# Weight sums in eight wide GpSimd operations a pair instead of twelve narrow ones, four exponential buffers, and scores issued two steps ahead of outputs

## The chip, the cores and the metric

The kernel runs on one core of a Trainium2 chip. The metric is the device time in microseconds (us) of one execution; for before it is the median of three runs, 595.99 us (595.43 to 596.42).

## The reference

Windowed attention with memory keys, followed by a two-layer feed-forward network, all in 32-bit floats:

```python
batch, n_heads, seq, head_dim = (4, 8, 768, 64)      # n_mem = 8
chunk, left_ctx, right_ctx = (32, 16, 8)
for c in range(seq // chunk):                        # 32 queries see 56 keys and 8 memory keys
    scores = scale * q_c @ k_full^T
    scores = scores - max(scores)
    a = exp(scores); a = a / (sum(a) + 1e-9)
    out[c] = a @ v_full
x = out.transpose(0, 2, 1, 3).reshape(3072, 512)
h = x @ w_in                                         # w_in 512 x 2048
g = max(h, 0) + alpha * min(h, 0)
return g @ w_out                                     # w_out 2048 x 512
```

## The kernel before, in words

**Blocks and units.** The 3072 tokens are eight blocks of 384. A block has four pairs of heads, and a (block, pair) is a *unit*; there are 32. A unit goes through: *scores* (TensorE, tile `s_ps`, L346), the row maximum (VectorE, `mx`, L369 and L372), six exponentials (ScalarE, `e`, L380), the denominator (VectorE, `den`, L395 and L398), a multiplication by its inverse (GpSimd, `e<-e,den`, L401), a ScalarE copy (`e2`, L405), fourteen 32-row transposes (VectorE, `pt`, L422), and *outputs* (TensorE, `a_ps`, L445), whose result becomes rows of x. Units 0 to 7 (blocks 0 and 1) go through a denser form of this at the start. The 24 others go two at a time, through the function `attend`.

**Full precision.** Every 32-bit factor of the feed-forward part is split into a rounded part ("high", a ScalarE copy) and the rest ("low", a subtraction), and a product is three TensorE products. So every hidden slice needs a `high` and a `low` before TensorE can use it.

**Places.** Blocks 0 and 1 are computed plainly. There are 32 *places*: one of the two blocks and one of the 16 slices f of the hidden width. A place has an `up` (12 products into `h_ps`, L760; two such buffers, so the `up` of place p needs place p-2 to have been read), a bend (ScalarE L769, then VectorE `g<-g,rise,h_ps`, L772), the split of the hidden slice (ScalarE `xh<-g` L778 and the subtraction `xl<-g,xh` or `gl<-g,gh`, L782), and a `down` (9 products into `o_ps`, L790). TensorE runs the `down` of a place after the `up` of the second place behind it. Places 0 to 17 alternate between the blocks, slices 0 to 8; place 18 is slice 9 of block 0, place 23 slice 14, place 24 slice 15; places 25 to 31 are slices 9 to 15 of block 1. Each slice's weights are first decoded, on ScalarE and VectorE: `w_t<-w_t` copies (L677) and shifts (L681), `a<-a,w_t` (L685), and the low part `w<-a,w` (L698), all 1024 elements a partition.

**Blocks 2 to 7** go in three big stages of two blocks. A 2x2 product is done with seven sub-products (L1139) of sums of blocks of x (`xf`; L931, L935, L949) and sums of blocks of w_in. The latter are made once, early, by `put_far`, on GpSimd, for each of the eight pairs of slices, and stored in device memory as `far_a` and `far_b`, with copies of the weights themselves; `load` brings them back for each stage. In `put_far` L870 adds high and low parts, L873 adds and subtracts quarters, ScalarE rounds (L877), L880 forms the low part, and SyncE stores.

**What sets the order.** Nothing is scheduled on the chip: each engine runs its own queue in order and waits on semaphores. The queues are written by a planner (`Plan`) when the program is built: each step is given an engine, a cost and a due time (`rest`), and the planner lists the steps by them. Costs and due times thus move instructions without changing what they do. `BEGIN` gives the places at which `attend` is called for units 8 and up, `AT_PAIR` and `AT_REST` the points in the big stages; `FIRST_SLOW` is the first place whose low part is made on GpSimd instead of VectorE.

Of the kernel before, what the change touches and what calls it, by code (L numbers as in the profile page):

```python
# [100 lines left out]
FIRST_SUM, SUM_EVERY = 9, 3  # L101
FIRST_SLOW = 20
# [8 lines left out]
DUE_WEIGHTS = 4  # L111
# [77 lines left out]
def body(ctx: ExitStack, tc: tile.TileContext, qvw, kw, whole, heads, w_in, w_out, alpha, out):  # L189
# [73 lines left out]

    def due(u, later=0):

        return rest(begins(u) + later + (5.5 if u >= FIRST_FRONT else 0))
# [4 lines left out]

    def e_keys(u):
        return [("e", u % 2, n) for n in range(NJ * 2)]

    def den_keys(u):
        return [("den", u % 3, n) for n in range(NJ * 2)]
# [83 lines left out]
    def scores(us):  # L360
# [57 lines left out]
    def turn(u):  # L418
# [125 lines left out]
    def windows(u):  # L544
# [20 lines left out]
        def total():  # L565
            st["den"] = sm.tile([P, NJ * 2, 1], F32, name="den", tag=f"den{u % 3}")
# [93 lines left out]
    def decode_part(k, parts):  # L660
# [52 lines left out]
        step(POOL if late else DVE, 1.3 if late else 0.15 + 0.53 * n, low, reads=[a] + [("w", i, f, 0) for i in parts],  # L713
# [16 lines left out]
    def hidden(blk, f, first_f, last_f):  # L730
# [72 lines left out]
        def add_bend():  # L803
# [3 lines left out]
            step(*((POOL, 1.05) if slow else (DVE, 0.56)), low, reads=[sd, gh], writes=[gl] + new)  # L807
# [21 lines left out]
    MORE = PLACES + [(sums, f"s{i}", [("f", i, 0), ("f", i, 1)]) for i in range(4)]  # L829
# [31 lines left out]
    def put_far(i, place):  # L861
        f0, f1 = 2 * i, 2 * i + 1
        t = {}

        def w(f, hl, k2):
            return ws[f, 0][:, hl, k2 * HALF:(k2 + 1) * HALF]

        def full(n, f, k2):
            t[n] = sums.tile([P, HALF], F32, name="sum", tag=f"t{n}")
            nc.gpsimd.tensor_tensor(out=t[n], in0=w(f, 0, k2).bitcast(F32), in1=w(f, 1, k2).bitcast(F32), op=ALU.add)  # L870

        def merge(n, a, b, op):
            nc.gpsimd.tensor_tensor(out=t[n], in0=t[a], in1=t[b], op=op)  # L873

        def high(n, x):
            t["s", x] = sums.tile([P, 2, HALF], F32R, name="form", tag=f"s{x}")
            nc.scalar.copy(out=t["s", x][:, 0], in_=t[n])  # L877

        def low(n, x):
            nc.gpsimd.tensor_tensor(out=t["s", x][:, 1], in0=t[n], in1=t["s", x][:, 0].bitcast(F32), op=ALU.subtract)  # L880

        def put(x, to):
            nc.sync.dma_start(out=to.rearrange("p (l m) -> p l m", l=2), in_=t["s", x].bitcast(F32))

        def raw_sum(n, f, k2):
            step(POOL, 0.7, partial(full, n, f, k2), reads=[("gate", place - 1), ("w", 0, f, 0), ("w", 0, f, 1)], writes=[("t", n)])

        def add(n, a, b, op):
            step(POOL, 0.7, partial(merge, n, a, b, op), reads=[("t", a), ("t", b)], writes=[("t", n)])

        def form(n, x, to, key):
            step(ACT, 0.4, partial(high, n, x), reads=[("t", n)], writes=[("f", x, 0), ("f", x, 1)])
            step(POOL, 0.7, partial(low, n, x), reads=[("t", n), ("f", x, 0)], writes=[("f", x, 1)])
            step(SP, 0.7, partial(put, x, to), reads=[("f", x, 0), ("f", x, 1)], writes=[key])
# [115 lines left out]
    def big(s):  # L1010
# [228 lines left out]
        def meet(u, banks):  # L1239
# [206 lines left out]
```

## Time and profile before

| what | value |
| --- | --- |
| median of three runs | 595.99 us |
| the profiled execution, its own time | 596.48 us |
| its span, first to last instruction | 594.7 us |
| TensorE busy | 575.0 us (97%) |
| VectorE busy | 456.5 us (77%) |
| ScalarE busy | 302.2 us (51%) |
| GpSimd busy | 201.7 us (34%) |
| mean granted TensorE clock | 0.991 |

In the profile PE is TensorE, PEld its weight loads, DVE VectorE, ACT ScalarE, POOL GpSimd, SP SyncE. A row of the timeline gives start, duration, engine, line, operation, tiles, shape and count, and in brackets the idle time before it with what ended it. The profiled execution lies 0.5 us above the median of the runs; 1.8 us of its time lie outside the span.

### The profile page before, as it was taken

The page shows a single profiled execution, that of the slowest core. Times are in us where ns is not written, and L with a number is a line of the kernel's source. Part 1 is how long each engine was busy: PE and PEld are TensorE (multiplying, and loading weights), DVE is VectorE, ACT ScalarE, POOL GpSimd, SP SyncE. Part 2 cuts the span into 40 slices and gives each one's busy share as a digit, 9 for nine tenths or more (in the row PEclk, how much of TensorE's full clock was granted, in tenths as well). Part 3 has the DMA queues.
Part 4 walks back from the last instruction along what each step waited for, and adds up shares of the span by engine and source line. Part 5 has one row for each costly group of instructions (what it writes and reads, how often), then busy time and mean ns, then how long its engine had stood idle before and what let it go on. Part 6 is the DMA issues. An engine that isn't in the chain of part 4 may idle for free.

```text
span 594.7 us, 12044 instructions
## 1 busy us (share of the span) xinstructions
PE 575.0 (97%) x4467; PEld 508.3 (85%) x4467; DVE 456.5 (77%) x987; ACT 302.2 (51%) x796; POOL 201.7 (34%) x230
## 2 busy tenths in 40 slices
PE   7999999769999999999999999999999999999997
PEld 4888987658988889999888998999888999999886
DVE  7989999878687978798879688897959466566420
ACT  3887878553765553534654633536464433323421
POOL 5663395997699460001123500101212500000000
PEclk9999999897999999999999999999999999999999
DMA  8999746384698577677898886778797776776821
GB/s 317 398 418 416 304 178 244 110 311 181 210 372 346 170 266 262 245 293 265 329 354 285 285 309 230 252 252 311 288 301 272 224 272 209 259 280 243 316 92 53
DMA packets 44395, 159.41 MB, mean 268 GB/s; under 512 B 5040, under 2 KB 10416, under 8 KB 35632
## 3 DMA queue, kind: packets, MB, share of 16 engines
q1 hardware_dynamic: 44192, 158.51, 73.0%
q8 instruction: 35, 0.57, 0.4%
q14 instruction: 24, 0.20, 0.1%
q10 hardware_dynamic: 144, 0.13, 0.1%
HBM read 129.26 MB, written 29.36 MB: 267 GB/s over the span
## 4 chain that ended last, share of the span: by engine, by line
PE 75%; POOL 5%; DVE 4%; issue 1%; ACT 1%; POOLq 0%; ACTq 0%
PE b_ps L1071 33%; PE b_ps L1139 27%; PE o_ps L790 4%; PE h_ps L760 4%; PE a_ps L445 3%; PE b_ps L1107 2%; PE s_ps L346 2%; POOL form L880 2%; POOL sum L870 2%; POOL sum L873 1%; DVE xf L935 1%; DVE w L698 1%; DVE w_t L677 0%; DVE a L685 0%; DVE pt L422 0%
## 5 line engine op out<-in xcount | busy, mean ns | idle before, releaser
L1139 PE MATMUL b_ps<-xf,wa 128*128 128x384 f32 x924 | 172.7, 336 | 0.1
L1139 PEld LDWEIGHTS b_ps<-xf,wa 128*128 128x128 f32 x924 | 161.9, 188 | 7.0 <-ACT plain L519 0.7
L1159 DVE TENSOR_TENSOR u<-b_ps,u 128x384 f32<-128x384 f32 x154 | 82.7, 554 | 37.5 <-PE b_ps L1139 33.6
L422 DVE STREAM_TRANSPOSE pt<-e 32x64 f32<-32x64 f32 (+1 forms) x336 | 99.5, 301 | 14.8 <-POOL e L401 9.1
L1032 ACT ACTIVATE g<-u 128x384 f32<-128x384 f32 x88 | 45.8, 525 | 102.5 <-DVE u L1159 98.6
L1071 PE MATMUL b_ps<-wo,xh 128*128 128x512 f32 x276 | 86.0, 393 | 0.0
L1071 PE MATMUL b_ps<-wo,gh 128*128 128x512 f32 x276 | 85.6, 392 | 0.0
L401 POOL TENSOR_TENSOR e<-e,den 128x384 f32<-128x384 f32 x24 | 20.4, 850 | 141.3 <-DVE den L398 137.1
L760 PE MATMUL h_ps<-xh,w 128*128 128x384 f32 x256 | 66.9, 343 | 0.0
L1071 PEld LDWEIGHTS b_ps<-wo,gh 128*128 128x128 f32 x276 | 51.8, 188 | 9.9
L1071 PEld LDWEIGHTS b_ps<-wo,xh 128*128 128x128 f32 x276 | 51.8, 188 | 9.7
L790 PE MATMUL o_ps<-w,xh 128*128 128x512 f32 x168 | 53.9, 403 | 0.0
L1071 PE MATMUL b_ps<-wo,gl 128*128 128x512 f32 x138 | 53.9, 390 | 0.0
L1071 PE MATMUL b_ps<-wo,xl 128*128 128x512 f32 x138 | 53.9, 390 | 0.0
L760 PE MATMUL h_ps<-xl,w 128*128 128x384 f32 x128 | 45.1, 352 | 5.6 <-DVE g L772 5.6
L380 ACT ACTIVATE e<-s_ps,mx 128x64 f32<-128x64 f32 x144 | 43.2, 319 | 10.9 <-DVE mx L372 10.9
L760 PEld LDWEIGHTS h_ps<-xh,w 128*128 128x128 f32 x256 | 47.4, 192 | 1.3 <-DVE w L698 0.6
L949 POOL TENSOR_TENSOR plain<-plain 128x384 f32<-128x384 f32 x24 | 26.7, 1137 | 46.0 <-ACT plain L519 45.4
L880 POOL TENSOR_TENSOR form<-sum,form 128x256 fp32r<-128x256 f32 x32 | 32.1, 1026 | 29.0 <-ACT form L877 29.0
L790 PE MATMUL o_ps<-w,xl 128*128 128x512 f32 x84 | 34.3, 408 | 5.1 <-DVE xl L782 5.1
L790 PEld LDWEIGHTS o_ps<-w,xh 128*128 128x128 f32 x168 | 32.8, 195 | 6.5
L1035 DVE SCALAR_TENSOR_TENSOR g<-g,rise,u 128x384 f32<-128x384 f32 x44 | 28.2, 641 | 10.8 <-ACT g L1032 10.3
(112 smaller groups left out, 928.4 us busy)
## 6 DMA issues: line engine op xcount, KB each, us to landing
wo<-far_o SPq DMA_DIRECT2D x46, 1024.0 KB, 4.8
wa<-far_a SPq DMA_DIRECT2D x22, 1024.0 KB, 4.8
wa<-far_b SPq DMA_DIRECT2D x22, 768.0 KB, 5.8
w_t<-w_in SPq DMA_DIRECT2D x16, 512.0 KB, 9.7
w_t<-w_out SPq DMA_DIRECT2D x16, 512.0 KB, 9.3
far_o<-w SPq DMA_DIRECT2D x16, 512.0 KB, 4.8
qk<-kw SPq DMA_DIRECT2D x24, 272.0 KB, 6.4
v_t<-qvw SPq DMA_DIRECT2D x24, 256.0 KB, 6.2
```

The source lines that it names most:

```text
L380: nc.scalar.activation(out=st["e"][:, i], in_=st["s"][h2][:, n], func=AF.Exp, scale=SCALE, bias=d["mx"][:, u - us[0], n, h2:h2 + 1], accum ...
L401: nc.gpsimd.tensor_tensor(out=st["e"], in0=st["e"], in1=st["den"].broadcast_to([P, NJ * 2, KW]), op=ALU.mult)
L422: nc.vector.transpose(out=pts[u % NPT][quad * CH:(quad + 1) * CH, j, t0:t0 + n1 - n0].rearrange("p t h q -> p (t h) q"), in_=(st["e"], zer ...
L760: nc.tensor.matmul(out=h["ps"][:, :BT], lhsT=ws[f, 0][:, wk, k * P:(k + 1) * P], rhs=parts(blk, k)[1](xk), start=(k == 0 and n == 0), stop ...
L790: nc.tensor.matmul(out=o_ps[tt], lhsT=h[gk][:, tt * P:(tt + 1) * P], rhs=ws[f, 1][:, wk], start=(f == first_f and i == 0), stop=(f == last ...
L880: nc.gpsimd.tensor_tensor(out=t["s", x][:, 1], in0=t[n], in1=t["s", x][:, 0].bitcast(F32), op=ALU.subtract)
L949: step(POOL, 0.95, lambda: nc.gpsimd.tensor_tensor(out=plain_at(to[0]), in0=plain_at(a[0]), in1=plain_at(b[0]), op=ALU.subtract), reads=[a ...
L1032: nc.scalar.activation(out=h[name], in_=src(), func=AF.Relu, scale=-1.0)
L1035: nc.vector.scalar_tensor_tensor(out=to() if to else h[name], in0=h[name], scalar=rise[:, f:f + 1], in1=src(), op0=ALU.mult, op1=ALU.add)
L1071: nc.tensor.matmul(out=o[which][tt], lhsT=h[gk][:, tt * P:(tt + 1) * P], rhs=w[:, wk].bitcast(F32R), start=(f == turns[which][0] and i == ...
L1139: nc.tensor.matmul(out=h[bank[1]][:, :BT], lhsT=weight(wk, p).bitcast(F32R), rhs=xf[xi][:, xk, p], start=p == 0 and k == 0, stop=p == 1 an ...
L1159: nc.vector.tensor_tensor(out=h[t], in0=h[bank[1]][:, :BT], in1=h[t if of is None else of], op=ALU.add)
```

## The change

**Weight sums.** For one pair of slices, GpSimd did twelve operations of 256 elements a partition: four sums of high and low parts, four sums of quarters, four low parts. Now the sums of high and low parts and the low parts are taken over both halves at once: two of 512, four of 256, two of 512. ScalarE rounds twice 512 instead of four times 256, and SyncE stores two forms instead of four. The forms lie elsewhere in `far_a` and `far_b`, so one sub-product (T1) takes its weights from the second load and another (B22) from the first.

**Places.** The sums of the eight pairs began at places 9, 12, 15, ... 30; now they begin at 9, 11, 13, 18, 22, 26, 29 and 30. `FIRST_SLOW` goes from 20 to 14, so the low parts of places 14 to 19 move from VectorE to GpSimd. Some of the planner's costs are larger than they were.

**Attention.** The exponentials of units 8 and up get four buffers instead of two (denominators four instead of three). Scores of two units are issued two steps ahead of the outputs (news are units v+4 and v+5 where the outputs are of v and v+1), not one. A new table `END` gives the places of the outputs; the weights and transposes are due with it. In the first big stage one of the four slices ahead of the second `attend` is taken before it, not two.

```diff
-BEGIN = (20, 24, 28, 32, 36, 40.3, 48.2, 55.8, 59.8, 69.4, 77.3, 85)
-AT_PAIR = ({2: 18, 5: 20}, {3: 26, 6: 28}, {})
-AT_REST = ({2: 22, 11: 24}, {2: 30, 11: 32}, {})
+BEGIN = (20, 22, 25.5, 28.5, 32, 36.0, 44, 49.5, 55.8, 58.8, 66.4, 75.3)
+END = (25, 28.5, 32.5, 38.5, 46.5, 49.5, 54.8, 58.5, 65.4, 75.3, 81.5, 92.5)
+AT_PAIR = ({2: 16, 5: 18}, {1: 24, 3: 26}, {})
+AT_REST = ({3: 20, 8: 22}, {4: 28, 12: 30}, {})
...
-FIRST_SUM, SUM_EVERY = 9, 3
-FIRST_SLOW = 20
+SUM_AT = (9, 11, 13, 18, 22, 26, 29, 30)
+SPLIT = 1
+FIRST_SLOW = 14
...
+    def e_place(u):
+        return u % 2 if u < NWIN else u % 4
...
-        step(DVE, 0.14 + 0.28 * n, ends, writes=r)
-        step(DVE, 0.15 + 0.54 * n, join, reads=r, writes=[a])
+        step(DVE, 0.14 + (0.28 if f < 6 else 0.35) * n, ends, writes=r)
+        step(DVE, 0.15 + (0.54 if f < 6 else 0.6) * n, join, reads=r, writes=[a])
...
-        raw_sum(0, f0, 0)
-        raw_sum(1, f1, 0)
-        step(POOL, 0.7, lambda: ... merge(2, 0, 1, ALU.subtract), ...)
-        form(2, 0, b[:, :2 * HALF], ("db", i, 1))
-        raw_sum(3, f1, 1)
-        add(1, 1, 3, ALU.add)
-        form(1, 1, a[:, 6 * HALF:], ("da", i, 1))
-        add(0, 1, 0, ALU.subtract)
-        form(0, 2, a[:, 4 * HALF:6 * HALF], ("da", i, 2))
-        raw_sum(3, f0, 1)
-        add(3, 3, 0, ALU.subtract)
-        form(3, 3, b[:, 4 * HALF:], ("db", i, 2))
+        raw_sum(0)
+        raw_sum(1)
+        add((1, 1), (1, 0), (1, 1), ALU.add)
+        add((1, 0), (0, 0), (1, 0), ALU.subtract)
+        form(1, b[:, :4 * HALF], ("db", i, 1))
+        add((0, 0), (1, 1), (0, 0), ALU.subtract)
+        add((0, 1), (0, 1), (0, 0), ALU.subtract)
+        form(0, a[:, 4 * HALF:], ("da", i, 1))
...
-        def meet(u, banks):
-            olds, news = [u - 2, u - 1], [u, u + 1] if u < NU else []
+        def meet(v, banks):
+            olds, news = [v, v + 1], [v + 4, v + 5] if v + 4 < NU else []
...
-            for f in BEFORE[:2]:
+            for f in BEFORE[:SPLIT]:
                 whole(0, f)
-            meet(16, None)
+            meet(14, None)
```

Behind the change a line has a number up to 16 higher: the bend L772 is L781, the hidden low part L782 is L791, the weights' L698 is L707, L681 is L690, L685 is L694, L677 is L686, the sums L870, L873 and L880 are L887, L890 and L898, L401 is L410, L422 is L431, L395 and L398 are L404 and L407.

First place: VectorE, in the decoding of the last slices. The queue of before, from the bend of place 16 to the low part of place 17:

```order
L772 SCALAR_TENSOR_TENSOR g<-g,rise,h_ps 128x384
L677 COPY w_t<-w_t 128x512
L782 TENSOR_TENSOR xl<-g,xh 128x384
L681 TENSOR_SCALAR w_t<-w_t 128x1024
L698 TENSOR_TENSOR w<-a,w 128x2x512
L772 SCALAR_TENSOR_TENSOR g<-g,rise,h_ps 128x384
L685 SCALAR_TENSOR_TENSOR a<-a,w_t 128x1024
L677 COPY w_t<-w_t 128x1024
L782 TENSOR_TENSOR xl<-g,xh 128x384
```

And of after, from the bend of place 16 (first row) over that of place 17 (fifth row) to that of place 18 (last row):

```order
L781 SCALAR_TENSOR_TENSOR g<-g,rise,h_ps 128x384
L707 TENSOR_TENSOR w<-a,w 128x2x512
L686 COPY w_t<-w_t 128x512
L690 TENSOR_SCALAR w_t<-w_t 128x1024
L781 SCALAR_TENSOR_TENSOR g<-g,rise,h_ps 128x384
L694 SCALAR_TENSOR_TENSOR a<-a,w_t 128x1024
L686 COPY w_t<-w_t 128x512
L690 TENSOR_SCALAR w_t<-w_t 128x1024
L781 SCALAR_TENSOR_TENSOR g<-g,rise,h_ps 128x384
```

The hidden low parts are gone from this queue, and the bends of places 16 to 18 stand ahead of more of the decoding: in before the weights' low part of slice 12 (the L698 row shown) and all of slice 12 lie ahead of the bend of place 17; in after that bend has only the low part of slice 11 and half of slice 12 ahead of it.

Second place: GpSimd, at about the same time; in before the end of the sums of slices 4 and 5 and the start of those of 6 and 7:

```order
L870 TENSOR_TENSOR sum<-w 128x256
L873 TENSOR_TENSOR sum<-sum 128x256 x2
L880 TENSOR_TENSOR form<-sum,form 128x256 x3
L870 TENSOR_TENSOR sum<-w 128x256 x2
L880 TENSOR_TENSOR form<-sum,form 128x256
L873 TENSOR_TENSOR sum<-sum 128x256
```

In after the start of the sums of slices 6 and 7, with the hidden low parts of places 17 (third row) and 18 (seventh row) among them:

```order
L887 TENSOR_TENSOR sum<-w 128x512
L887 TENSOR_TENSOR form<-w 128x512
L791 TENSOR_TENSOR xl<-g,xh 128x384
L890 TENSOR_TENSOR form<-form 128x256
L890 TENSOR_TENSOR form<-sum,form 128x256
L890 TENSOR_TENSOR sum<-form,sum 128x256
L791 TENSOR_TENSOR xl<-g,xh 128x384
```

So TensorE's `down` products now wait for GpSimd's queue here, and the sums are fewer and wider.

Third place: VectorE, at the first units that go through `attend` (units 8 and 9). Before, from the denominators to the bend of place 21:

```order
L698 TENSOR_TENSOR w<-a,w 128x2x512
L395 TENSOR_SCALAR den<-den 128x6
L398 RECIPROCAL den<-den 128x6
L422 STREAM_TRANSPOSE pt_975<-e 32x192 x4
L395 TENSOR_SCALAR den<-den 128x6
L422 STREAM_TRANSPOSE pt_975<-e 32x192
L772 SCALAR_TENSOR_TENSOR g<-g,rise,h_ps 128x384
```

After, up to the bend of place 22 (last row):

```order
L407 RECIPROCAL den<-den 128x6
L431 STREAM_TRANSPOSE pt_975<-e 32x192
L781 SCALAR_TENSOR_TENSOR g<-g,rise,h_ps 128x384
L365 MEMSET s_ps 32x2x16
L378 TENSOR_REDUCE mx<-s_ps 128x6
L707 TENSOR_TENSOR w<-a,w 128x2x512
L365 MEMSET s_ps 32x2x16
L378 TENSOR_REDUCE mx<-s_ps 128x6
L781 SCALAR_TENSOR_TENSOR g<-g,rise,h_ps 128x384
```

The bend of place 21 now has one transpose ahead of it instead of five; the other transposes come behind the low part of slice 15. The maxima of the next two units (L378) follow at once.

More of the change, by code (lines that the diff above doesn't have):

```diff
@@ L262, in begins, with ends @@
         return u // NPAIR if u < NWIN else BEGIN[(u - NWIN) // 2]
+    def ends(u):
+        return END[(u - NWIN) // 2]
     def due(u, later=0):
-        return rest(begins(u) + later + (5.5 if u >= FIRST_FRONT else 0))
+        return rest(begins(u) + later)
     def sets(u):
         return u % NKB
+    def e_place(u):
+        return u % 2 if u < NWIN else u % 4
     def e_keys(u):
-        return [("e", u % 2, n) for n in range(NJ * 2)]
+        return [("e", e_place(u), n) for n in range(NJ * 2)]
     def den_keys(u):
-        return [("den", u % 3, n) for n in range(NJ * 2)]
+        return [("den", u % 4, n) for n in range(NJ * 2)]
     def load_unit(u):
@@ L806, in add_bend @@
             step(*((ACT, 0.51) if place < HIGH_ACT else (DVE, 0.35)), high, reads=[sd], writes=[gh] + new)
-            step(*((POOL, 1.05) if slow else (DVE, 0.56)), low, reads=[sd, gh], writes=[gl] + new)
+            step(*((POOL, 1.05) if slow else (DVE, 0.75 if place > 6 else 0.56)), low, reads=[sd, gh], writes=[gl] + new)
         def add_down(o_ps):
@@ L828, in body @@
     PLACES = [(tmp, f"o{NTT + i}", [("tmp", NTT + i)]) for i in range(2)]
-    MORE = PLACES + [(sums, f"s{i}", [("f", i, 0), ("f", i, 1)]) for i in range(4)]
+    MORE = PLACES + [(sums, "r", [("rs", 0, 0), ("rs", 0, 1)])]
+    MORE += [(sums, f"s{i}", [("f", i, 0), ("f", i, 1)]) for i in range(2)]
     def leave_at(late):
@@ L862, in put_far @@
         f0, f1 = 2 * i, 2 * i + 1
[L863 to L894, printed above, removed]
+        r, t = [None, None], [None, None]
+        gate = [("gate", place - 1)]
+        def part(n, k2):
+            return r[n][:, k2 * HALF:(k2 + 1) * HALF]
+        def formed(n):
+            t[n] = sums.tile([P, 2, 2 * HALF], F32R, name="form", tag=f"s{n}")
@@ new lines, in full, with merge, high @@
+        def full(n):
+            w = ws[f0 + n, 0].bitcast(F32)
+            if n:
+                formed(n)
+            r[n] = t[n][:, 1].bitcast(F32) if n else sums.tile([P, 2 * HALF], F32, name="sum", tag="r")
+            nc.gpsimd.tensor_tensor(out=r[n], in0=w[:, 0], in1=w[:, 1], op=ALU.add)
+        def merge(to, a, b, op):
+            nc.gpsimd.tensor_tensor(out=part(*to), in0=part(*a), in1=part(*b), op=op)
+        def high(n):
+            if not n:
+                formed(n)
+            nc.scalar.copy(out=t[n][:, 0], in_=r[n])
@@ new lines, in low, with put, raw_sum, add @@
+        def low(n):
+            nc.gpsimd.tensor_tensor(out=t[n][:, 1], in0=r[n], in1=t[n][:, 0].bitcast(F32), op=ALU.subtract)
+        def put(n, to):
+            nc.sync.dma_start(out=to.rearrange("p (l m) -> p l m", l=2), in_=t[n].bitcast(F32))
+        def raw_sum(n):
+            step(POOL, 1.4, partial(full, n), reads=gate + [("w", 0, f0 + n, 0), ("w", 0, f0 + n, 1)],
+                 writes=[("rs", n, 0), ("rs", n, 1)] + ([("f", n, 1)] if n else []))
+        def add(to, a, b, op):
+            step(POOL, 0.9, partial(merge, to, a, b, op), reads=[("rs",) + a, ("rs",) + b], writes=[("rs",) + to])
@@ L896, in put_far, with form @@
+        def form(n, to, key):
+            step(ACT, 0.65, partial(high, n), reads=[("rs", n, 0), ("rs", n, 1)], writes=[("f", n, 0)] + ([] if n else [("f", n, 1)]))
+            step(POOL, 1.4, partial(low, n), reads=[("rs", n, 0), ("rs", n, 1), ("f", n, 0)], writes=[("f", n, 1)])
+            step(SP, 0.7, partial(put, n, to), reads=[("f", n, 0), ("f", n, 1)], writes=[key])
         a, b, o = far_a[i], far_b[i], far_o[i]
         step(SP, 0.7, lambda: nc.sync.dma_start(out=a[:, :4 * HALF].rearrange("p (l m) -> p l m", l=2), in_=ws[f0, 0].bitcast(F32)),
-             reads=[("gate", place - 1), ("w", 0, f0, 0), ("w", 0, f0, 1)], writes=[("da", i, 0)])
@@ L1008, in keep_place @@
         return None, ("gs", f)
+    fresh = []
     def big(s):
@@ L1351, in body @@
             decode(f)
-        i, late = divmod(PLACE[blk, f] - FIRST_SUM, SUM_EVERY)
-        if not late and 0 <= i < NFP:
-            put_far(i, PLACE[blk, f])
+        if PLACE[blk, f] in SUM_AT:
+            put_far(SUM_AT.index(PLACE[blk, f]), PLACE[blk, f])
         if (blk, f) == (0, CLEAR):
```

77 lines of the change are left out of this document (36 added, 41 removed).

## The prediction

> **What bounds the kernel now.** I read the windows first (where TensorE is not busy), then TensorE's waits, then its timeline at each wait, then the chain and the queues of VectorE and GpSimd around it. The windows' columns are busy us of PE, PEld, DVE, ACT and POOL, granted clock, DMA share and GB/s:
>
> ```profile
> 57.76:100.00 42.24, 41.33 (x205) 36.31 (x204) 41.83 (x48) 34.78 (x50) 24.23 (x21) 1.00 0.59 232
> 100.00:140.00 40.00, 30.24 (x312) 26.58 (x311) 33.65 (x46) 21.27 (x60) 37.08 (x35) 0.88 0.68 250
> 140.00:220.00 80.00, 78.83 (x762) 70.32 (x762) 62.23 (x174) 46.86 (x174) 58.24 (x71) 1.00 0.70 252
> 220.00:260.00 40.00, 39.96 (x325) 36.82 (x324) 34.24 (x84) 17.05 (x53) 3.63 (x4) 1.00 0.69 252
> ```
>
> From 220 us on TensorE never waits, so buffers and lead there can gain nothing. What can be gained is 0.91 us (42.24 - 41.33) up to 100 us, 9.76 us of idle TensorE plus a clock of 0.88 up to 140, and 1.17 up to 220. The waits say on whom, and the timeline how long and at what speed TensorE went on:
>
> ```profile
> PE h_ps L760 <- DVE g L772: 5.6, 1, 5.6
> PE o_ps L790 <- DVE xl L782: 5.1, 2, 4.2
> PE b_ps L1107 <- DVE plain L1035: 1.2, 1, 1.2
> ...
> 110.06 0.79 PE L790 MATMUL o_ps<-w,xl 128*128 128x512 f32 x1 [4.20 <-DVE xl L782]
> 113.62 0.33 PE L760 MATMUL h_ps<-xl,w 128*128 128x384 f32 x1
> ...
> 127.65 1.25 PE L346 MATMUL s_ps<-qk 64*32 64x64 f32 x96
> 134.46 0.69 PE L760 MATMUL h_ps<-xl,w 128*128 128x384 f32 x1 [5.56 <-DVE g L772]
> ...
> 134.46 4.21 PE h_ps L760 x12
> 138.67 4.98 PE o_ps L790 x18
> 143.65 2.10 PE h_ps L760 x12
> 145.75 4.12 PE o_ps L790 x18
> ```
>
> The last four rows are of the chain. An `up` takes 2.10 us and two `down` 4.12 at full clock, but 4.21 and 4.98 behind the long wait: 2.97 us lost to the clock. Behind the first wait one `down` takes 113.62 - 110.06 = 3.56 against 2.06, another 1.50. So the first stall costs 5.7 us and the second 8.5. The wait of 1.2 us leaves the clock at 1.00 (its window is not slower), so I charge short waits no clock. The Trainium skill (TensorE: Matmul & The Clock Gate, What's actually happening) says that the array falls to half clock after an idle window of about 3.4 us; the two long waits here, over that, lost clock, and the short one did not.
>
> What stands behind the waits: the first `down` is that of place 17, whose low part VectorE ended at 108.96 + 1.05. The second is the third `up` behind place 20, held by the bend of place 21:
>
> ```profile
> 108.96 1.05 DVE L782 TENSOR_TENSOR xl<-g,xh 128x384 fp32r<-128x384 f32 x1
> ...
> 130.93 1.51 DVE L422 STREAM_TRANSPOSE pt<-e 32x192 f32<-32x192 f32 x4 [3.68 <-POOL e L401]
> 132.47 0.88 DVE L395 TENSOR_SCALAR den<-den 128x6 f32<-128x6 f32 x1
> 133.79 0.61 DVE L772 SCALAR_TENSOR_TENSOR g<-g,rise,h_ps 128x384 f32<-128x384 f32 x1
> ...
> 129.39 0.72 POOL L870 TENSOR_TENSOR sum<-w 128x256 f32<-128x256 f32 x1
> 130.07 0.83 POOL L401 TENSOR_TENSOR e<-e,den 128x384 f32<-128x384 f32 x1
> ```
>
> VectorE stood 3.68 us in front of the first transpose, because GpSimd had sums ahead of the multiplication. So the stage is bounded by the two together: VectorE without a gap, and GpSimd behind with its sums.
>
> They also slow each other. The groups between 61.4 and 139 us, then rows of the same operations while the other engine rests or works:
>
> ```profile
> L880 POOL TENSOR_TENSOR form<-sum,form 128x256 fp32r<-128x256 f32 x18 | 22.1, 1248 | 24.8 <-ACT form L877 24.8
> L870 POOL TENSOR_TENSOR sum<-w 128x256 f32<-128x256 f32 x16 | 18.9, 1190 | 0.3
> L873 POOL TENSOR_TENSOR sum<-sum 128x256 f32<-128x256 f32 x16 | 17.0, 1062 | 1.0
> L782 POOL TENSOR_TENSOR xl<-g,xh 128x384 fp32r<-128x384 f32 x2 | 2.0, 1001 | 0.0
> ...
> L698 DVE TENSOR_TENSOR w<-a,w 128x1024 fp32r<-128x1024 f32 x10 | 16.2, 1623 | 0.0
> L782 DVE TENSOR_TENSOR xl<-g,xh 128x384 fp32r<-128x384 f32 x12 | 11.1, 929 | 0.1
> ...
> L698 DVE TENSOR_TENSOR w<-a,w x14: 1218/1746/1976, 39.7 to 135.5; 128x1024 fp32r<-128x1024 f32 x14
> L698 POOL TENSOR_TENSOR w<-a,w x4: 1277/1302/1502, 20.6 to 38.2; 128x512 fp32r<-128x512 f32 x4
> ...
> 36.28 0.55 DVE L782 TENSOR_TENSOR xl<-g,xh 128x384 fp32r<-128x384 f32 x1
> 84.02 1.09 DVE L782 TENSOR_TENSOR xl<-g,xh 128x384 fp32r<-128x384 f32 x1
> 29.46 1.64 DVE L782 TENSOR_TENSOR xl<-g,xh 128x384 fp32r<-128x384 f32 x1
> 29.36 1.32 POOL L698 TENSOR_TENSOR w<-a,w 128x512 fp32r<-128x512 f32 x1 [1.77 <-ACT w L693]
> ```
>
> A subtraction on VectorE takes 0.55 us alone, 1.09 beside GpSimd's 256-wide operations, 1.64 beside a 512-wide one: it waits about 0.54 or 1.09 us, the length of what GpSimd is doing. GpSimd's 256-wide operations take 0.72 alone and 1.06 to 1.25 here.
>
> **The change part by part.**
>
> *Weight sums.* Elements a pair are the same (3072); eight starts instead of twelve. Alone: 12 x 0.72 = 8.6 us against 4 x 1.30 + 4 x 0.72 = 8.1, little. In this stage: 12 x 1.17 (mean of the three groups) = 14.0 us; a 512-wide one beside VectorE shows in no row, so its bounds are 1.30 (alone) and 1.30 + 0.53 = 1.83 (the excess of L880, 1.25 - 0.72). I take 1.7, near the upper end since VectorE is never idle: 4 x 1.7 + 4 x 1.06 = 11.0. GpSimd gains 3 us a pair. For VectorE a wide operation is a wait twice as long, half as often: no gain, no loss. ScalarE saves two copies and SyncE two stores a pair; neither is on the path.
>
> *Low parts of places 14 to 19 to GpSimd.* Of the three low parts of places 14 to 16 that stood ahead of the bend of place 17, VectorE is rid of at least 3 x 0.5, at most 3 x 0.93; I take 1.8 us. The bend of place 17 also no longer stands behind the end of slice 12 and the start of 13, which the queue of before has ahead of it:
>
> ```profile
> 99.17 1.64 DVE L685 SCALAR_TENSOR_TENSOR a<-a,w_t 128x1024 int32<-128x1024 int32 x1
> 101.26 0.77 DVE L677 COPY w_t<-w_t 128x512 int16<-128x512 int16 x1
> 102.81 1.23 DVE L681 TENSOR_SCALAR w_t<-w_t 128x1024 int32<-128x1024 int32 x1
> 103.97 1.76 DVE L698 TENSOR_TENSOR w<-a,w 128x1024 fp32r<-128x1024 f32 x1
> 105.65 0.60 DVE L772 SCALAR_TENSOR_TENSOR g<-g,rise,h_ps 128x384 f32<-128x384 f32 x1
> ```
>
> That is 5.4 us more. So it comes as soon as TensorE has done the `up`, about 100 us. Then GpSimd decides. I follow its queue from 66 us, when ScalarE lets the first form go in both kernels (it must, it is the same place in ScalarE's queue), to the low part of place 17: 12 wide operations, 9 narrow, 4 low parts of places 14 to 17, and about 6 us in which it waits for ScalarE's roundings: 12 x 1.7 + 9 x 1.06 + 4 x 1.01 + 6 = 40, so 106 us. TensorE, without earlier loss, wants it at 104. Of the first stall's 5.7 us, 2 stay as a wait too short for the clock. The bounds: 0 stays at 1.5 us a wide operation, all of it at 2.0 (12 x 0.3 = 3.6 more). The same queue makes the low part of place 14 about 1.4 us late, while the 0.9 us lost up to 100 us goes: +0.5.
>
> *Sums pulled ahead.* GpSimd idles 18 us between 57.76 and 100 us and will idle some 6: it works 12 us more beside the decoding. VectorE's excess from the L782 and L698 rows is 12 x 0.38 + 10 x 0.40 = 8.6 us for about 61 us of GpSimd; 0.14 us a us; at most it is 0.75, if every 0.72 us of GpSimd makes VectorE wait 0.54. I take 0.2, since the decode's copies and shifts swell too: 2.4 us. By its queue the bend of place 14 has a lead of about 1.9 us over TensorE, so +0.5; at the upper end 7 us.
>
> *Second stall.* The bend of place 21 now has one transpose ahead of it, which needs one multiplication, and that has two wide sums and a narrow one just ahead of it on GpSimd. What I find late is the low part of place 20 on GpSimd, behind that multiplication (1.2 us), and the low part of slice 14, behind bend and maximum (about 1 us). Of 8.5 us 2.5 stay. The bend of place 23 comes behind 20 transposes:
>
> ```profile
> L422 DVE STREAM_TRANSPOSE pt<-e 32x192 f32<-32x192 f32 x168 | 61.9, 368 | 12.3 <-POOL e L401 9.1
> L422 DVE STREAM_TRANSPOSE pt<-e 32x64 f32<-32x64 f32 x168 | 37.6, 233 | 2.5
> ```
>
> Eleven wide and nine narrow take 6.1 us, and I find TensorE 1 us early. Bounds for both together: 0, and the whole 8.5.
>
> *Four buffers, scores two steps ahead, END.* Behind 220 us nothing waits, so nothing is gained; the exponentials' place among ScalarE's work is covered by its 17 busy us of 40. Cost if the cover goes: the last outputs of the second big stage now have 9 products of `down` (6.2 us) behind them instead of 12; I charge 0, at most 1.5. At 213 us the outputs come ahead of nine chunks instead of six: of 1.17 us 0.3 stays.
>
> *Sum.* -5.7 + 2 + 0.5 + 0.5 - 8.5 + 2.5 + 1 - 1.2 + 0.3 = -8.6 us. The span becomes 586.1, with the 1.8 outside it 587.9 against 596.48 for the profiled execution. The median of the runs is 0.5 us lower: 587.4, say 587.
>
> **The rivals.**
>
> *GpSimd becomes the bound: slower.* The low parts of places 14 to 31 all stand in one queue with wide sums. At 2.0 us a wide operation the first stall is back whole; that is the point from which it decides. At 2.2 the `down` of place 17 starts 2.2 us later than before; nine more wide operations up to the multiplication cost the second stall another 2, with nothing won there: about 600 us. For it: GpSimd is busy 37.08 of 40 us. Against: the worst mean row is 0.53 us of excess, which gives 1.83.
>
> *The two share a port and nothing is won: the same.* If a VectorE operation and a GpSimd one simply excluded each other, a low part moved from 0.55 us of VectorE to 1.01 of GpSimd (a row beside VectorE's transposes) would load the shared thing more, by 6 x 0.46 = 2.8 us, and the stage would stay as long: 596 to 598. Against it: GpSimd stood idle 24.8 us waiting for ScalarE in this stretch, so the shared thing is not full. The Trainium skill (GPSIMD Engine Reference, Specifications) has the rule: GpSimd's interfaces to on-chip memory are shared with VectorE, contention arising with instructions of two such inputs. The trace agrees, with 0.55, 1.09 and 1.64 us; by that rule alone the move is a loss.
>
> *Half won.* The first stall goes, the second comes back as a wait for another multiplication or bend: -8.6 + 5 = about 592.5.
>
> *All stalls go* (each remainder 0): -16.3, so 580.
>
> **How the numbers follow.** This kernel's measurement can tell about 0.2% (1.2 us) from no change. Forecast, 582 to 591: 0.56. Half won, 591 to 594.7: 0.15. Better than 582: 0.05. The same, by the shared port: 0.09. Slower, by GpSimd: 0.15. Faster 0.76, same 0.09, slower 0.15. The range takes in half won, the same and the near part of slower: 581.5 to 597.5.
>
> **What would show it.** Right: TensorE's wait for the hidden low part and for the bend under 3 us each, the granted clock at 1.00 between 100 and 140 us, the first `up` behind 140 us some 9 us earlier; GpSimd's wide sums at 1.5 to 1.8 us; the stage from 220 us on as long as before. Wrong: wide sums at 2 us or more; TensorE waiting on GpSimd's low part for over 5 us; or waits in the big stages, at the last outputs of one.

## The result

The changed kernel is slower: 603.1 us (median of six runs, 600.67 to 606.27) against 596.2 us for the kernel before on the same chip (595.41 to 596.88), a ratio of 1.0121 with an interval of 1.0090 to 1.0153. Forecast were 587 us and a range that ended at 597.5. The ratios here and below follow the means of the runs and not their medians, so the two can differ by up to 1 us.

The profiled execution took 602.57 us, 600.8 of them its span. The windows of the changed kernel, with the columns of those of before (busy us of PE, PEld, DVE, ACT and POOL, granted clock, DMA share, GB/s):

```profile
57.76:100.00 42.24, 39.90 (x199) 35.56 (x199) 41.26 (x41) 30.87 (x42) 29.79 (x20) 1.00 0.61 240
100.00:140.00 40.00, 34.00 (x339) 29.45 (x339) 37.12 (x52) 27.43 (x79) 37.01 (x26) 0.96 0.53 193
140.00:220.00 80.00, 74.51 (x813) 64.83 (x813) 61.66 (x173) 44.00 (x163) 52.35 (x53) 0.96 0.71 256
```

From 100 to 140 us TensorE's idle time shrinks from 9.8 to 6.0 us and the clock rises from 0.88 to 0.96. That was forecast. But from 140 to 220 us TensorE, which lacked 1.2 us before, now lacks 5.5 and runs at 0.96. TensorE's waits say on whom (us in total, times, longest):

```profile
PE o_ps L799 <- POOL xl L791: 12.2, 5, 5.5
...
PE o_ps L799 <- DVE xl L791: 1.6, 1, 1.6
...
PE b_ps L1087 <- DMA wo<-far_o: 1.1, 2, 0.9
```

Its timeline gives the three longest waits:

```profile
110.25 0.79 PE L799 MATMUL o_ps<-w,xl 128*128 128x512 f32 x1 [2.84 <-POOL xl L791]
...
132.05 0.50 PE L799 MATMUL o_ps<-w,xl 128*128 128x512 f32 x1 [2.82 <-POOL xl L791]
...
182.68 0.80 PE L799 MATMUL o_ps<-w,xl 128*128 128x512 f32 x1 [5.49 <-POOL xl L791]
```

And the chain (start, us, what) leads from the third to a store:

```profile
138.59 2.10 PE h_ps L769 x12
...
166.25 10.89 DMA far_b<-form
...
182.68 7.14 PE o_ps L799 x18
```

The `up` that started at 143.65 before starts at 138.59: 5.1 us are won up to here. Then two `down`, 4.12 us at full clock, wait 5.49 us and take 7.14: 8.5 us. The first plain product of block 2 starts at 193.4 us instead of 188.5, so the lead of 5.1 has become a lag of 4.9. Of that 10.0, 8.5 are this stall; the rest I did not follow further. The first pair product lags 4.1 us (221.9 against 217.8), and behind it three short waits (0.85 us for a maximum of VectorE, 0.91 and 0.20 for loads `wo<-far_o`) bring the lag at the end to 6.1.

The stall is read from GpSimd's own waits, its timeline, and SyncE's timeline ahead of it (SPq is its queue, in which it issues transfers):

```profile
POOL form L887 <- DMA far_b<-form: 13.7, 3, 7.5
```

```profile
168.39 1.29 POOL L887 TENSOR_TENSOR sum<-w 128x512 f32<-128x512 f32 x1
177.21 1.26 POOL L887 TENSOR_TENSOR form<-w 128x512 f32<-128x512 f32 x1 [7.52 <-DMA far_b<-form]
...
180.95 0.72 POOL L890 TENSOR_TENSOR sum<-sum 128x256 f32<-128x256 f32 x1
181.63 0.99 POOL L791 TENSOR_TENSOR xl<-g,xh 128x384 fp32r<-128x384 f32 x1
```

```profile
162.43 0.38 SPq L1013 DMA_DIRECT2D wa<-far_a  x1
...
163.83 0.71 SPq L1013 DMA_DIRECT2D wa<-far_b  x1
165.84 0.32 SPq L1013 DMA_DIRECT2D wa<-far_a  x1
166.25 0.73 SPq L901 DMA_DIRECT2D far_b<-form  x1
```

The raw sum of a pair's second slice is written into the low half of a *form* tile (`r[n] = t[n][:, 1]` in `full`). That tile is the one from which the pair before is still being stored. So this sum waits for the store of the pair before, and GpSimd's queue, which is worked off in order, keeps four sums and then the hidden low part behind it; ScalarE had that low part's rounding done at 174.5 us. The store was issued at 166.25, directly behind two loads of 1 MB and one of 0.75 MB, and landed 10.89 us later, where the median of such a store is 3.0. The trace's landings say why: the three loads, and a store of 256 KB between them, landed 4.2, 4.8, 7.1 and 9.6 us after the issue of this store, in the order of their issue, and it landed 1.3 us behind the last of them. Stores of the same kind with no transfer under way ahead of them landed in 2.6 us in the same trace. No run moved the loads, so this rests on the order in the traces.

### The profile page after: what moved, and what is told of

The parts are those of the page before. It is cut to its first block, busy times and chain, and to the rows that moved or that the text cites. A ratio compares the mean times of both kernels' runs of the same rounds, so it can differ in the third digit from the quotient of the medians.

```text
span 600.8 us, 11949 instructions
## 1 busy us (share of the span) xinstructions
PE 577.4 (96%) x4467; PEld 508.1 (85%) x4467; DVE 460.8 (77%) x981; ACT 300.3 (50%) x780; POOL 202.6 (34%) x204
## 4 chain that ended last, share of the span: by engine, by line
PE 77%; POOL 9%; DMA 7%; DVE 3%; issue 2%; ACT 1%; POOLq 0%; SPq 0%; DVEq 0%; ACTq 0%
PE b_ps L1087 29%; PE b_ps L1152 27%; PE o_ps L799 6%; PE h_ps L769 5%; PE b_ps L1123 3%; DMA wo<-far_o 3%; DMA far_b<-form 3%; PE a_ps L454 2%; POOL form L898 2%; PE s_ps L355 2%; POOL xl L791 1%; PE a_ps L614 1%; POOL form L890 1%; POOL form L887 1%; POOL sum L890 1%
## 5 line engine op out<-in xcount | busy, mean ns | idle before, releaser
L431 DVE STREAM_TRANSPOSE pt<-e 32x192 f32<-32x192 f32 (+1 forms) x336 | 100.5, 302 | 16.5 <-PE a_ps L454 7.9
L769 PE MATMUL h_ps<-xh,w 128*128 128x384 f32 x256 | 65.4, 336 | 0.0
L410 POOL TENSOR_TENSOR e<-e,den 128x384 f32<-128x384 f32 x24 | 21.7, 922 | 116.2 <-ACT e L389 81.8
L1087 PEld LDWEIGHTS b_ps<-wo,gl 128*128 128x128 f32 x138 | 25.9, 188 | 7.7 <-issue 1.9
```

The source lines that it names most:

```text
L410: nc.gpsimd.tensor_tensor(out=st["e"], in0=st["e"], in1=st["den"].broadcast_to([P, NJ * 2, KW]), op=ALU.mult)
L431: nc.vector.transpose(out=pts[u % NPT][quad * CH:(quad + 1) * CH, j, t0:t0 + n1 - n0].rearrange("p t h q -> p (t h) q"), in_=(st["e"], zer ...
L769: nc.tensor.matmul(out=h["ps"][:, :BT], lhsT=ws[f, 0][:, wk, k * P:(k + 1) * P], rhs=parts(blk, k)[1](xk), start=(k == 0 and n == 0), stop ...
L1087: nc.tensor.matmul(out=o[which][tt], lhsT=h[gk][:, tt * P:(tt + 1) * P], rhs=w[:, wk].bitcast(F32R), start=(f == turns[which][0] and i == ...
```

## The experiments

T1 is this store wait; T2 says that GpSimd has too much to do and the store wait only falls into it; T3 that the six moved low parts do the harm; T4 that the new order of scores does.

### The raw sum in a tile of its own (e1)

```diff
-            if n:
-                formed(n)
-            r[n] = t[n][:, 1].bitcast(F32) if n else sums.tile(..., tag="r")
+            r[n] = sums.tile(..., tag=f"r{n}" if n else "r")
...
-            if not n:
-                formed(n)
+            formed(n)
```

(Two small constant tiles share buffers with others, to make room, here and in e4 to e6, e8, e9 and e11.) In the two traces every engine runs the same instructions in the same order; only the tile is another.

> The changed kernel, but the raw sum of a pair's second slice has a tile of its own, and not the low half of the form tile that the pair before is still storing from. T1 (the store wait): GpSimd's waits for far_b<-form (3.41, 7.52 and 2.77 us) go; TensorE's stall at 182.68 us (5.49, and 3.0 of clock) goes, and that at 110 (2.84, and 1.6 of clock) loses about 3: 603.1 - 8.5 - 3 = 591.5, between 588 and 595, and the runs scatter less than the 1% of the changed kernel. T2 (GpSimd has too much to do, the store wait only falls into it): the hidden low parts stay late, 599 to 604.

594.95 us, ratio 0.9987 (0.9969 to 1.0005): 8.2 us of the 603.1 are gone, and the time cannot be told from that of the kernel before. The window of 140 to 220 us is full again, and the hidden low part follows the sums at once, at 175.50 instead of 181.63:

```profile
140.00:220.00 80.00, 79.94 (x862) 71.37 (x861) 67.59 (x189) 47.05 (x170) 59.21 (x60) 1.00 0.79 289
```

```profile
73.58 2.00 POOL L895 TENSOR_TENSOR form<-sum,form 128x512 fp32r<-128x512 f32 x1 [2.18 <-ACT form L892]
...
169.34 2.53 POOL L885 TENSOR_TENSOR sum<-w 128x512 f32<-128x512 f32 x2
171.95 3.19 POOL L888 TENSOR_TENSOR sum<-sum 128x256 f32<-128x256 f32 x4
175.50 1.01 POOL L791 TENSOR_TENSOR xl<-g,xh 128x384 fp32r<-128x384 f32 x1 [0.36 <-ACT xh L787]
```

Two parts of T1's expectation failed. The stall at 110 us stayed (2.89 us): where the first store wait (3.41 us, up to 72.55) was, GpSimd now waits 2.18 us for ScalarE's rounding, which stands at the same place of ScalarE's queue. And the runs scatter as before (592.85 to 600.12).

### Both raw sums in form tiles (e7)

```diff
-            if n:
-                formed(n)
-            r[n] = t[n][:, 1].bitcast(F32) if n else sums.tile(..., tag="r")
+            formed(n)
+            r[n] = t[n][:, 1].bitcast(F32)
```

> The suspected cost doubled: the changed kernel with the raw sums of both slices in the form tiles. The orders of TensorE, VectorE and SyncE are those of the changed kernel. The first raw sum of a pair now waits for the store that was issued last. T1: GpSimd's waits for a store grow from 13.7 to some 20 to 35 us, and the time to 605 to 615. T2 (the store wait only falls into time that GpSimd lacks anyway): 601 to 604.

613.51 us, ratio 1.0308 (1.0281 to 1.0334). GpSimd's waits for stores and its timeline at the longest:

```profile
POOL form L886 <- DMA far_a<-form: 32.0, 7, 10.3
POOL form L886 <- DMA far_b<-form: 2.8, 1, 2.8
```

```profile
185.54 2.50 POOL L886 TENSOR_TENSOR form<-w 128x512 f32<-128x512 f32 x2 [10.29 <-DMA far_a<-form]
188.11 3.13 POOL L889 TENSOR_TENSOR form<-form 128x256 f32<-128x256 f32 x4
191.20 1.00 POOL L791 TENSOR_TENSOR xl<-g,xh 128x384 fp32r<-128x384 f32 x1
```

34.8 us of waits instead of 13.7, and 10.4 us more time, with the same pattern: four sums and then the hidden low part behind the wait. Again every engine runs the instructions of the changed kernel in the same order. With e1 this settles T1 against T2 for that order: 0, 13.7 and 34.8 us of store waits go with 595, 603 and 613.5 us.

### The moved low parts (e2, e5), and each half of the change (e3, e4)

In the changed kernel (e2), and with the tile of e1 (e5):

```diff
-FIRST_SLOW = 14
+FIRST_SLOW = 20
```

> The changed kernel with the low parts of places 14 to 19 back on VectorE. T1 (store wait): the low part of place 17 is no longer behind it, but that of the stall at 182.68 us is on GpSimd in the kernel before too, so 8.5 us of loss stay; VectorE's own stall near 110 us comes back in part: 600 to 606. T3 (the six moved low parts do the harm): the stalls near 110 and 132 us (2.84 + 1.6 + 2.82) go, 594 to 597.

> As e1 (raw sum in its own tile), and the low parts of places 14 to 19 back on VectorE. With the store wait gone the moved low parts can be judged. If they are the harm that is left (T3), the waits of e1 on GpSimd's low parts near 90 to 110 us (1.08 + 0.72 + 0.31 + 2.89) and at 131 (3.27, and 1.0 of clock) go for the most part: 587 to 591. If VectorE only takes GpSimd's place as the one that is late, which e2 beside the changed kernel speaks for (603.4 against 603.1): 594 to 599.

603.42 us, ratio 1.0133 (1.0107 to 1.0160), as T1 expected, and 598.81 us, 1.0040 (1.0026 to 1.0054). T3 falls: without the store wait the moved low parts are worth 3.9 us of gain (3.2 by the ratios) at the places and costs of the changed kernel.

The sums alone in the kernel before (e3), and everything but the sums (e4). e3 takes of the change only what stands in `put_far` and in the reading of its forms, e4 all but that. One place of each, seen from the changed kernel, e3 first:

```diff
-        if PLACE[blk, f] in SUM_AT:
-            put_far(SUM_AT.index(PLACE[blk, f]), PLACE[blk, f])
+        i, late = divmod(PLACE[blk, f] - FIRST_SUM, SUM_EVERY)
...
-        raw_sum(0)
-        raw_sum(1)
+        raw_sum(0, f0, 0)
+        raw_sum(1, f1, 0)
```

> The kernel before with the weights' sums of the changed kernel alone (eight operations, two form tiles, the raw sum in one of them; a pair every three places as before; scores, exponentials and low parts as before). T1: the store wait comes here too, 2 to 8 us at several pairs, and with it TensorE's waits for hidden low parts: 599 to 607. T4 (the new order of scores and outputs does the harm, not the sums): 594 to 597.

> The changed kernel with the weights' sums of the kernel before (twelve operations of 256 wide, four sum tiles, four form tiles); the new places of the pairs, order of scores, four exponentials and low parts from place 14 stay. T1: GpSimd no longer waits for a store, the stall at 182.68 us goes: 588 to 595. T2 (GpSimd has too much to do): four more operations a pair, about 3 us a pair more: 604 or more. T4 (the order of scores does the harm): 600 to 604.

599.03 us, ratio 1.0048 (1.0029 to 1.0066), and 599.5 us, 1.0054 (1.0036 to 1.0072): each half alone makes the kernel slower. The first lies in T1's range. It shows store waits of 6.1 us, the longest 2.3, but no wait of TensorE on GpSimd's low part, so it does not speak for T1 alone. The second missed T1's expectation and lies between it and T4's: no store wait, but GpSimd's low parts are late all the same (9.9 us in three waits). Something else also makes them late, so the next runs took up the order.

### The planner told what things take (e6, e8 to e12)

The planner reckoned a wide sum or low half at 1.4 us and a hidden low part on GpSimd at 1.05. The groups of the changed kernel between 61.4 and 139 us (busy us, mean ns; the last row is the dearest of four narrow groups, which together mean 1.25 us):

```profile
L791 POOL TENSOR_TENSOR xl<-g,xh 128x384 fp32r<-128x384 f32 x9 | 13.2, 1464 | 0.0
L898 POOL TENSOR_TENSOR form<-form 128x512 fp32r<-128x512 f32 x5 | 8.4, 1683 | 17.6 <-ACT form L895 17.6
L898 POOL TENSOR_TENSOR form<-sum,form 128x512 fp32r<-128x512 f32 x4 | 8.3, 2083 | 0.2 <-ACT form L895 0.2
L887 POOL TENSOR_TENSOR sum<-w 128x512 f32<-128x512 f32 x4 | 7.7, 1920 | 0.2
L887 POOL TENSOR_TENSOR form<-w 128x512 f32<-128x512 f32 x4 | 6.6, 1638 | 3.4 <-DMA far_b<-form 3.4
L890 POOL TENSOR_TENSOR sum<-form,sum 128x256 f32<-128x256 f32 x4 | 6.1, 1519 | 0.2
```

Only numbers change; for e1 (then e6) and for the changed kernel itself (then e12):

```diff
-            step(POOL, 1.4, partial(full, n), ...)
+            step(POOL, 2.0, partial(full, n), ...)
...
-            step(POOL, 0.9, partial(merge, to, a, b, op), ...)
+            step(POOL, 1.1, partial(merge, to, a, b, op), ...)
...
-            step(POOL, 1.4, partial(low, n), ...)
+            step(POOL, 2.1, partial(low, n), ...)
...
-            step(*((POOL, 1.05) if slow else (DVE, 0.75 ...)), low, ...)
+            step(*((POOL, 1.45) if slow else (DVE, 0.75 ...)), low, ...)
```

> As e1, with the planner's costs for GpSimd set to what the trace of e1 shows: wide sums and low halves 2.0 and 2.1 us (they stood at 1.4), narrow ones 1.1 (0.9), hidden low parts 1.45 (1.05). The instructions are the same, their order is another. Theory Q (the order: at 104.4 us two wide raw sums of 1.97 us each stand ahead of the low part of place 17 because the planner takes them for 1.4): the stalls of e1 at 109.75 (2.89) and 131.46 (3.27 and 1.0) go, 587 to 591. Rival L (the load: GpSimd is busy 36.6 of 40 us there, any order is late somewhere): 593 to 598.

> The changed kernel itself (raw sum in the form tile) with the true costs of e6 in the planner, orders of TensorE, VectorE and SyncE as in e6. If the store wait stands by itself, whatever the order: GpSimd waits for far_b<-form again, and the time is 5 to 10 us over e6: 599 to 605. If an order made with true costs gives the store the time that it needs: 594 to 597.

594.6 us, ratio 0.9976 (0.9965 to 0.9986), and 594.87 us, 0.9977 (0.9966 to 0.9989). The first lies in the range of rival L, the second in that of an order that gives the store its time.

One thing about e12: the planner knows the raw sum and the low half by two names, though in the changed kernel they are the same bytes, so nothing but the costs keeps them in order. In the changed kernel the order comes out right in all eight pairs. In e12 one pair has its low half made ahead of the last use of the raw sum there, so two sums of that pair, and with them the output, are not those of the reference. Its time can still be compared: its instructions are those of e6, in the same order on every engine.

For e1 the true costs change nothing that can be told: the stalls at 110 and 131 us shrink to 1.1 and 1.1 + 1.2, and others come. For the changed kernel they are worth 8.2 us, as much as the tile of its own, against what I expected of a wait that stands by itself. Its waits and two places of GpSimd's timeline:

```profile
POOL form L887 <- DMA far_b<-form: 13.7, 3, 8.8
```

```profile
167.94 1.30 POOL L887 TENSOR_TENSOR form<-w 128x512 f32<-128x512 f32 x1 [2.81 <-DMA far_b<-form]
169.19 1.03 POOL L791 TENSOR_TENSOR xl<-g,xh 128x384 fp32r<-128x384 f32 x1
...
228.04 1.30 POOL L887 TENSOR_TENSOR form<-w 128x512 f32<-128x512 f32 x1 [8.80 <-DMA far_b<-form]
229.42 0.75 POOL L890 TENSOR_TENSOR form<-form 128x256 f32<-128x256 f32 x1
```

GpSimd waits 13.7 us for stores, exactly as long as in the changed kernel. But the longest wait lies at 219 to 228 us, with sums behind it and no hidden low part, and the low part right behind the wait of 2.81 us still comes in time: TensorE waits once for a low part of GpSimd in this run, 1.8 us at 104 to 106 us. So it is not the wait that costs: it is a hidden low part behind the wait that TensorE wants before it is done.

The same with narrow sums, in e4 (then e8) and in the kernel before with nothing else changed (e10, which also takes over the changed kernel's costs for VectorE):

```diff
-            step(POOL, 0.7, ...)
+            step(POOL, 1.15, ...)
...
-            step(*((POOL, 1.05) if slow else ...), low, ...)
+            step(*((POOL, 1.45) if slow else ...), low, ...)
```

> As e4 (twelve narrow sums, new order of scores), with the planner's costs set to what the traces show: narrow sums 1.15 us (they stood at 0.7), hidden low parts 1.45 (1.05). Theory Q: the stalls of e4 at 97.89 (2.55), 113.14 (4.56 and 1.6 of clock), 134.92 (2.77) shrink to a half or less: 591 to 595. Rival L: 597 to 602.

> The kernel before with the planner's costs alone set to what the traces show (narrow sums 1.15 us, hidden low parts 1.45, VectorE's costs as in the changed kernel); tables, buffers, sums as before. If the true costs are what makes e8 fast, whatever the order of scores: 589 to 592. If the new tables (scores two steps ahead, places of the pairs, low parts from place 14) carry e8: 594 to 598.

590.15 us, ratio 0.9901 (0.9889 to 0.9913), a little under theory Q's range, and 592.11 us, 0.9930 (0.9916 to 0.9944), at the upper edge of the first range. True costs alone take 4.0 us off the kernel before. Under true costs the parts of the change can be told apart with two more: e8 with `FIRST_SLOW` at 20 (e11),

> As e8, with the low parts of places 14 to 19 back on VectorE. With true costs and no store wait, what the move of the six low parts is worth. If it is worth what the prediction took (VectorE rid of 1.8 us ahead of the first stall, and the bend of place 17 no longer behind a slice): 593 to 597. If it is worth nothing: 589 to 591.5.

589.36 us, ratio 0.9885 (0.9871 to 0.9898), the fastest of all, so the move is worth nothing here (its longest wait left is one of 4.2 us, for a low part of GpSimd at 126 us); and e6 with each form stored in two halves to where the kernel before has them (e9):

```diff
-        form(1, b[:, :4 * HALF], ("db", i, 1))
+        form(1, [(b[:, :2 * HALF], ("db", i, 1)), (a[:, 6 * HALF:], ("da", i, 1))])
...
-        form(0, a[:, 4 * HALF:], ("da", i, 1))
+        form(0, [(a[:, 4 * HALF:6 * HALF], ("da", i, 2)), (b[:, 4 * HALF:], ("db", i, 2))])
...
-            product(b, 1, w(1, HALF), "T1")
+            product(b, 0, w(0, 6 * HALF), "T1")
...
-            product(a, 0, w(0, 5 * HALF), "B22")
+            product(a, 1, w(1, 4 * HALF), "B22")
```

> As e6 (own tile, true costs, 512-wide sums), but each form is stored in two halves to where the kernel before has them, so that a pair's weights lie as in e8, and T1 and B22 read the tiles that they read before; GpSimd's order is that of e6. It splits the 4.4 us between e6 (594.6) and e8 (590.15), of which 3.6 lie behind the first pair product (376.2 against 372.6 us from there to the end), with short waits for wo<-far_o. Theory Y (the places of the weights: the 1 MB tile is read until the last product of a pair, so its load starts later): 590.5 to 592.5. Rival W (the 512-wide operations do it): 594 to 596.

592.2 us, ratio 0.9936 (0.9923 to 0.9948), within theory Y's range. From one kernel to the next, one part of the change each, with true costs in all but the last (e1 to e8 and e9 to e12 ran on two chips, on which the kernel before takes 596.1 us alike):

| kernel | us | step |
| --- | --- | --- |
| e10: before | 592.11 | |
| e11: new tables, four exponentials, pairs' new places | 589.36 | -2.75 |
| e8: low parts of places 14 to 19 on GpSimd | 590.15 | +0.8 (intervals overlap) |
| e9: sums and low halves 512 wide, in two form tiles instead of four | 592.2 | +2.05 |
| e6: forms stored whole, T1 and B22 from the other load | 594.6 | +2.4 |
| e12: raw sum in the form tile | 594.87 | +0.3 (intervals overlap) |
| the changed kernel: the planner's old costs | 603.1 | +8.2 |

The first step is seen in TensorE's waits at the first big stage; e10, then e11:

```profile
PE b_ps L1071 <- DVE gl L1051: 1.7, 1, 1.7
PE b_ps L1107 <- DVE plain L1035: 1.5, 1, 1.5
```

```profile
PE b_ps L1118 <- DVE plain L1046: 0.5, 1, 0.5
```

So the new order of scores, which T4 blamed, is a gain under true costs. The third step shows in VectorE's decoding between 61.4 and 139 us, in e8 and then in e9:

```profile
L694 DVE SCALAR_TENSOR_TENSOR a<-a,w_t 128x1024 int32<-128x1024 int32 x10 | 15.5, 1550 | 0.0
L707 DVE TENSOR_TENSOR w<-a,w 128x1024 fp32r<-128x1024 f32 x10 | 14.6, 1455 | 0.7 <-ACT w L702 0.7
```

```profile
L694 DVE SCALAR_TENSOR_TENSOR a<-a,w_t 128x1024 int32<-128x1024 int32 x10 | 17.6, 1755 | 0.1
L707 DVE TENSOR_TENSOR w<-a,w 128x1024 fp32r<-128x1024 f32 x10 | 16.6, 1669 | 0.1
```

The two take 34.2 us beside the wide operations and 30.1 beside the narrow ones. They also grow in the two other pairs of kernels that differ only in the sums and what belongs to them: from 29.5 to 30.5 us (before and e3) and from 29.9 to 32.4 (e4 and the changed kernel). It is not the width alone, though: in e2 and e5, with wide sums but the low parts of places 14 to 19 on VectorE, they take 30.3 and 29.6. And one group by itself says little: the low parts took 1623 ns beside narrow sums in the kernel before and 1577 beside wide ones in the changed kernel. TensorE waits 3.7 us for VectorE's bends and weights in e9 (2.5 and 1.2) and not at all in e8, and 1.1 us for GpSimd's low parts instead of 3.1.

The fourth step lies mostly behind the first pair product (from there to the last product 376.2 us in e6, 374.2 in e9). The loads of e6 and then of e9 (KB each, median us from issue to landing):

```profile
wo<-far_o SPq DMA_DIRECT2D x46, 1024.0 KB, 7.2
wa<-far_a SPq DMA_DIRECT2D x22, 1024.0 KB, 8.5
wa<-far_b SPq DMA_DIRECT2D x22, 768.0 KB, 4.3
```

```profile
wo<-far_o SPq DMA_DIRECT2D x46, 1024.0 KB, 6.0
wa<-far_a SPq DMA_DIRECT2D x22, 1024.0 KB, 4.8
wa<-far_b SPq DMA_DIRECT2D x22, 768.0 KB, 6.5
```

With B22 reading it, the 1 MB tile is in use up to the last product of a pair. So its next load is issued behind that of the 0.75 MB tile in most pairs of e6, and ahead of it in e9 (for one pair of the second big stage SyncE's timeline has the 1 MB load at 350.81 us and the other at 348.37 in e6, and at 345.92 and 350.12 in e9). The 1 MB load then takes 3.7 us longer to land in e6, the other 2.2 us less. TensorE waits 1.4 us in all for `wo<-far_o` in e6, and not at all in e9; the rest of the 2.4 us was not followed.

## Why the prediction was wrong

**The step that failed first** is "ScalarE saves two copies and SyncE two stores a pair; neither is on the path". The count was right, the tiles were not looked at. Before, raw sums had tiles of their own and four form tiles served a pair; after, a raw sum is made in a form tile, so a store stands in GpSimd's queue ahead of it, and the longest of these waits, 7.52 us, was on the chain that ended last. I weighed what the operations take, and not what the written tile was last used for. It cost 8.2 us in the order of the changed kernel (e1), and 0.3 in another (e12). That is about half of the 15.7 us between forecast and result: without the store wait e1 still takes 594.95 us, where 587.4 were forecast. Of the other half, 2.4 us are the first stall (next paragraph) and 2.4 the new places of the weights; the rest was not taken apart.

**The wide sums** were taken at 1.7 us with bounds of 1.30 and 1.83. The four groups give 31.0 us for 17, 1.82, at the upper end. The row I priced the hidden low parts by (1.01) was far off: 1.46. The sums of quarters were taken at 1.06; their four groups together mean 1.25. In the stretch of the first stall's sum, from 66.2 us to the low part of place 17, the twelve wide operations took 23.4 us (1.95 each) instead of 20.4, the nine narrow ones 11.1 instead of 9.5, the four low parts 6.1 instead of 4.0, and the waits 3.4 (for a store) instead of 6 (for ScalarE): 44.0 us instead of 40, so the low part ended at 110.2 and not at 106. Of that stall 4.4 us were left (2.84, and 1.6 of clock), not 2.

Beyond the size the step was wrong too. By the stage's means a pair costs GpSimd 12.3 us instead of 14.0, so GpSimd gained 1.7 and not 3; but with true costs wide sums are 2 us slower than narrow ones (e8, e9), and no gain. "For VectorE a wide operation is a wait twice as long, half as often" did not hold: in three pairs of kernels the two largest groups of its decoding took longer beside wide sums, by 1.0, 2.5 and 4.1 us. The Trainium skill (SBUF — State Buffer, SBUF: two separate sides) has the port pair of the two as an exclusive lock, held for the whole instruction; the trace agrees, with the 0.55, 1.09 and 1.64 us that the prediction shows. That the width makes no difference in sum was my own inference, and it fails.

**The second stall** came as forecast: 2.82 us on the low part of place 20, forecast 2.5. That it came so near is in part luck: e1, with the same order of instructions, shows 3.27 us there and a clock of 0.66 behind it. The 1 us forecast for the bend of place 23 did not come, as TensorE waits for no bend. The wait at 213 us went, as forecast.

**Up to 100 us** I charged 0.5 for the low part of place 14 and 0.5 for the bend; there TensorE's idle time grew from 0.9 to 2.3 us, so 1.4. The sum is near, its parts are not: the wait for GpSimd was 0.71 us, and the one for VectorE, which was to go, grew from 0.87 to 1.63.

**From 220 us on** nothing was to happen, at most 1.5 us; it lost 2.0. The new places of the weights were described in the change and priced nowhere: 2.4 us. The new tables were charged 0; under true costs they are worth 2.75.

**The rivals.** "GpSimd becomes the bound" named the right engine and nearly the time (about 600), but by a wide sum of 2.0 to 2.2 us; the runs show a wait and its place in the queue instead, so the nearness of the time is luck. The sign to look for, TensorE waiting over 5 us on GpSimd's low part, was there (5.49).

## What to carry to other kernels

When a change lets one tile serve two ends, list for each write what last read the tile, transfers too, and what stands behind that write in its engine's queue: the price is that of the queue behind, not of the wait. Give such a tile one name in whatever orders the steps, so that no order can break it. In a kernel ordered by a table of costs, measure those costs again in the stage where they decide (beside the other engine's work, not alone) before judging any change of order; here that was worth more than any part of the change (2.75 us at best) in three of four kernels: 9.4 us from e4 to e8, 8.2 from the changed kernel to e12, 4.0 from the kernel before to e10, and nothing that can be told from e1 to e6. And price where the data lies, not only what makes it: which tile is read last sets when its next load can start.

## What the hardware showed

How much clock a wait costs did not follow its length. Windows of e3 (TensorE was busy up to 105.29 us, then came a wait of 1.94 us, which ends at 107.23), and of e1 behind a wait of 2.89:

```profile
104.00:107.00 3.00, 1.29 (x8) 0.97 (x6) 3.00 (x3) 1.91 (x3) 2.92 (x3) 1.00 0.95 371
107.00:110.70 3.70, 3.47 (x9) 2.30 (x9) 3.70 (x5) 0.58 (x2) 3.54 (x3) 0.64 1.02 416
```

```profile
109.75:112.20 2.45, 2.45 (x11) 2.04 (x12) 2.45 (x4) 0.52 (x1) 2.37 (x2) 1.00 0.08 28
```

The shorter wait was followed by a clock of 0.64, the longer one by 1.00; in the changed kernel 2.84 us cost 1.6 and 2.82 none. The Trainium skill (TensorE: Matmul & The Clock Gate, What's actually happening) puts the fall behind an idle window of about 3.4 us that runs on its own clock; a free phase would fit that like waits differ, but the falls behind 1.94 and 2.84 us lie under its figure. So my rule that waits under 3 us cost no clock does not hold.
